# Two of four wq loads split into eight-row transfers and wider, fewer instructions around them, in a GQA decode and Mish layer on one Trainium2 core

## The chip, the cores and the metric

The kernel runs on one core of a Trainium2 chip. The metric is the time of one execution on the device in microseconds (us), as the median of some runs. PE is TensorE, DVE VectorE, ACT ScalarE, POOL GpSimd, SP SyncE; PEld stands for the weight loads of PE. The 16 DMA engines of the core bring all data from HBM.

## The reference, cut to what matters

The layer adds the input, a grouped-query attention over a cache, and a dense layer with Mish. One token for each of 8 batches, 512 features, 32 query heads over 8 heads of keys and values (4 queries each), 8192 cached positions, heads of 128, all in float32.

```python
xn = layernorm(x)                                  # x [8, 1, 512]
q = (xn @ wq).reshape(B, 1, 32, 128)               # wq [512, 4096]
k, v = repeat(k_cache, 4, axis=1), repeat(v_cache, 4, axis=1)   # [8, 8, 8192, 128] each
p = softmax(einsum("bhqd,bhkd->bhqk", q, k) * 128 ** -0.5)
a = einsum("bhqk,bhkd->bhqd", p, v).reshape(B, 1, 4096) @ wo    # wo [4096, 512]
h = xn @ w1 + b1                                   # w1 [512, 1792]
return x + a + (h * tanh(softplus(h))) @ w2        # w2 [1792, 512]
```

The caches are 268 MB each, so nearly all of the 561 MB that are read are keys and values.

## The kernel before

**Items and buffers.** The work is a list of items, each with a load and a function that works on the loaded tile. `buffer()` hands out four tiles of 128 x 32 KB (`BUFS = 4`), and the main loop at the end of the kernel calls the load of item i + 3 (`AHEAD = 3`) before it works on item i. All big loads are issued on SP, in this order; each waits until its buffer is free, that is until PE has read the item four places before. `load_rows` (L104) gives every partition one contiguous run, 32 KB for a k or v item (4 MB in all), 16 KB for a wq or wo item (2 MB). x_sb (8 rows of 2 KB) and b1_sb (4 rows of 1792 B) are loaded by ACT at the start.

**The order.** A pack p is half of the batches (`PB = 4`) of one key head: 16 packs. The list begins with wq item 0, then k items of pack p alternate with v items of pack p - 1. w1 comes after the second k item, three more wq items at the third batch of packs 2, 6 and 10, wo items between packs, and at the end w2 in three parts with the last wo item in two parts between them. `after(k, f)` puts f off by k steps; a step is a `yield` of an item, so small work on PE falls between the parts of the big items. PE, DVE and POOL each run their instructions in program order.

**What an item does.** A wq item i projects the queries of the key heads n = 2i and 2i + 1: `project` runs 16 small matmuls for each n (L271; 8 columns of weights, 128 of data, the four query heads into four groups of 32 partitions of H), `spread_q` scales and spreads q (L284), transposes it by matmuls against psel (L294) and copies it to qc (L301). `expand` masks it by row group into the block matrix qT (L319). `scores` multiplies qT with a k tile into S (L359; 32 MATMUL records of 128x512 for an item, each float32 matmul being recorded as two), and in the last batch of a pack takes the maximum (L370). `maximum` and `weights` turn S into exponents (L413), which two transposes on DVE bring to pt (L422). `values` multiplies pt with a v tile (L450) into one of two O banks by the parity of the batch, and DVE picks the diagonal blocks with four instructions per batch (L460 once, L462 three times), masks in isel. `merge` sums groups of rows (L477) and divides (L481), `turn` transposes the result of one head by 16 matmuls (L499) and copies it to oW (L507), and `outputs` multiplies oW with a wo tile (L530) and adds to acc (L540); for the last pair of heads it adds into H instead. `mish` and `down` (L597) are the dense layer; `down` adds into H. The last instructions add H and acc into res (L752) and store it (L753).

Of the kernel before, what the change touches and what calls it, by code (L numbers as in the profile page):

```python
# [60 lines left out]
QR = CC  # L61
OR = 4
# [9 lines left out]
def kernel(  # L72
# [76 lines left out]
    O = [psum.tile([P, 512], F32, name=f"o{i}") for i in range(2)]  # L149
# [7 lines left out]

    psel = const.tile([P, REP, B], F32, name="psel")
# [12 lines left out]

    half = const.tile([P, 2], F32, name="half")
    qT = [const.tile([P, PB * (QB + 1)], F32, name=f"qT{i}") for i in range(QBUFS)]
    qc = const.tile([P, 4, KR, REP, B], F32, name="qc")
    qc0 = const.tile([P, KA, REP, B], F32, name="qc0")

    xnT = const.tile([P, QR, B], F32, name="xnT")
    xw = const.tile([P, W1R, 2, B], F32, name="xw")
    acc = const.tile([P, P], F32, name="acc")
    aT = const.tile([P, 2 * W2R, Q], F32, name="aT")  # L180

    def setup():
# [5 lines left out]
        for o in O:  # L188
            nc.vector.memset(o, 0.0)

        st = const.tile([B, 8], F32, name="st")
        scratch = work.tile([P, TG, NH, P], F32, name="e", bufs=1).rearrange("p t s f -> p (t s f)")
# [19 lines left out]
        nc.vector.tensor_copy(xnT.rearrange("p r b -> p (r b)"), M[:, : QR * B])  # L212
# [4 lines left out]
        nc.vector.tensor_copy(psel, ident.rearrange("p (h q) -> p h q", h=REP)[:, :, :B])  # L217
# [17 lines left out]
        nc.vector.tensor_scalar(far, far, FAR, -FAR, op0=ALU.mult, op1=ALU.add)  # L235

# [9 lines left out]
        return wide  # L246
# [17 lines left out]
    q_at = [H[:, 384:512], H[:, 256:384]]  # L264

    def project(n, w):

        for r in range(QR):
            for h in range(REP):
                at = r * BW + (n % 2 * REP + h) * DH  # L270
                nc.tensor.matmul(  # L271
                    q_at[n % 2][Q * h : Q * h + B, :],
                    xnT[:, r, :],
                    w[:, at : at + DH],
                    start=(r == 0),
                    stop=(r == QR - 1),
                )

    def spread_q(n, k, copies, dst):

        qs = work.tile([P, KR * P], F32, name="qs", bufs=1)[:, : k * P].rearrange(
            "p (r g i) -> p r g i", r=k, g=copies
        )
        nc.vector.tensor_scalar_mul(  # L284
            qs,
            q_at[n % 2]
            .rearrange("p (i r o) -> p r o i", r=k, o=1)
            .to_broadcast([P, k, copies, DH // k]),
            DH**-0.5,
        )  # L290

        def transposed():
            for r in range(k):
                nc.tensor.matmul(  # L294
                    H[:, r * R : (r + 1) * R],
                    qs[:, r].rearrange("p g i -> p (g i)"),
                    psel.rearrange("p h b -> p (h b)"),
                    start=True,
                    stop=True,
                )  # L300
            nc.vector.tensor_copy(  # L301
                dst, H[:, : k * R].rearrange("p (r h b) -> p r h b", r=k, h=REP)
            )

        return transposed

    def expand(p):


        n, hb = divmod(p, NP)  # L310
        t = qT[p % QBUFS]
        if p > 0:
            t = t.rearrange("p (b c) -> p b c", b=PB)[:, :, :QB]
            t = t.rearrange("p b (r q) -> p b r q", r=KR)
            q = qc[:, n % 4, :, :, hb * PB : (hb + 1) * PB].rearrange("p r h b -> p b r h")
            for j in range(NB):
                g, s = divmod(j, NH)
                lo = g * R + s * PB
                nc.vector.tensor_scalar(  # L319
                    t[:, :, :, lo : lo + R - U + 1 : U], q, bsel[:, j : j + 1], None, op0=ALU.mult  # L320
                )
# [55 lines left out]
    def maximum(p):  # L377
# [10 lines left out]
        nr2 = work.tile([1, REP, NH, PB], F32, name="nr2")  # L388
        for s in range(NH):
            nc.vector.tensor_copy(nr2[:, :, s, :], nb)  # L390
        nx = NX[p] = work.tile([1, G, R], F32, name="nx")
        nc.vector.tensor_copy(
            nx,
            nr2.rearrange("p h s b -> p (h s b)")
            .rearrange("p (o q) -> p o q", o=1)
            .to_broadcast([1, G, R]),
        )

    def weights(p):
# [3 lines left out]
        nc.tensor.transpose(M[:, 128:129], NX.pop(p).rearrange("p g q -> p (g q)"), ident[:1, :1])  # L403
# [16 lines left out]
        half = TG // 2  # L420
        for i in range(2):
            nc.vector.transpose(  # L422
                pt.rearrange("p (m t r) -> p t m r", m=TW, t=TG)[:, half * i : half * (i + 1)],
                e.rearrange("p t s (q m) -> p t m (s q)", m=TW)[:, half * i : half * (i + 1)],
            )
# [16 lines left out]
    def values(p, b, vt):  # L442
# [16 lines left out]
        os = OS[p, b] = work.tile([P, DH], F32, name="os", bufs=3)  # L459
        nc.vector.tensor_scalar(os, o[:, :DH], isel[:, 0:1], None, op0=ALU.mult)  # L460
        for i in range(1, W4):
            nc.vector.scalar_tensor_tensor(  # L462
                os,
                o[:, DH * i : DH * (i + 1)],
                isel[:, i : i + 1],
                os,
                op0=ALU.mult,
                op1=ALU.add,
            )
# [3 lines left out]
    def merge(p, b):  # L473
# [4 lines left out]
        if b == PB - 1:  # L478
            if hb == 0:
                oT[n] = work.tile([P, REP, B], F32, name="oT")  # L480
            nc.vector.tensor_mul(  # L481
                oT[n][:, :, hb * PB : (hb + 1) * PB],
# [3 lines left out]
            if hb == NP - 1:  # L486
                after(1, lambda: turn(n))

    def turn(n):


        if n % 2 == 0:
            oW[n] = work.tile([P, OR, 2, B], F32, name="oW")
        to = oW[n - n % 2]
        o = oT.pop(n)
        for k in range(2):
            j = n % 2 * 2 + k
            for r in range(OR):
                nc.tensor.matmul(  # L499
                    M[Q * j : Q * (j + 1), 384 + r * 2 * B : 384 + (r + 1) * 2 * B],  # L500
                    ident[:, r::OR],
                    o[:, 2 * k : 2 * k + 2, :].rearrange("p h b -> p (h b)"),
                    start=True,
                    stop=True,
                )
        rows = slice(n % 2 * 64, n % 2 * 64 + 64)
        nc.vector.tensor_copy(  # L507
            to[rows].rearrange("p r h b -> p (r h b)"), M[rows, 384 : 384 + OR * 2 * B]
        )

    def outputs(n, w, lo=0, hi=OR):


        last = n == HKV - 2
        to = H[:, :P] if last else M[:, 256:384]
        if n == 0:

            for g in range(G):
                nc.tensor.matmul(
                    to[Q * g : Q * g + B, :],  # L520
                    ident[:B, :B],
                    x_sb[:, g * P : (g + 1) * P],
                    start=True,
                    stop=False,
                )
        for r in range(lo, hi):
            for h in range(2):
                for g in range(G):
                    at = r * BW + h * D + g * P
                    nc.tensor.matmul(  # L530
                        to[Q * g : Q * g + B, :],
                        oW[n][:, r, h, :],
                        w[:, at : at + P],
                        start=(r == 0 and h == 0 and 0 < n and not last),
                        stop=(r == OR - 1 and h == 1 and not last),
                    )
        if n == 0:
            nc.vector.tensor_copy(acc, to)
        elif not last:
            nc.vector.tensor_add(acc, to, acc)  # L540

    def mish(w1_sb):
# [29 lines left out]
        one = work.tile([P, FG], F32, name="mo", bufs=1)  # L572
# [20 lines left out]
    def down(lo, hi, w):  # L593
        for j in range(2 * lo, 2 * hi):
            for g in range(G):
# [5 lines left out]
                    start=(j == 0),  # L601
# [17 lines left out]
    def wq_item(i):  # L619
        def spread(n):  # L620
            return spread_q(n, KR, NB, qc[:, n % 4])

        def work_on(t):
            project(2 * i, t)
            if i == 0:

                first = spread_q(0, KA, KA, qc0)
                project(1, t)
                first()

                def rest():
                    spread(0)()
                    after(1, lambda: spread(1)())

                after(2, rest)
            else:
                project(2 * i + 1, t)
                even = spread(2 * i)

                def then():  # L640
                    even()
                    after(1, spread(2 * i + 1))

                after(2, then)
# [166 lines left out]
```

## Time and profile before

| | |
|---|---|
| median of 3 runs | 1317.86 us (1317.59 to 1318.09) |
| the profiled execution | 1317.59 us, of which the profile's span is 1315.7 us |
| instructions in the profile | 11664: PE 5268 MATMUL and 5268 LDWEIGHTS, DVE 679 |
| busy | PE 1197.2 us (91%), DVE 275.5 us (21%), ACT 40.1 us (3%), POOL 10.9 us (1%) |
| DMA | 561.82 MB, 427 GB/s on average; 325 in the last of 40 slices |
| mean granted TensorE clock | 0.984 |

How to read it: matmuls are pipelined, so the mean duration of one (L359: 606 ns) is more than its share of the busy time (868.7 us for 1920). A chip's DMA engine works through packets, here of 4 to 32 KB; the records of the packets name their queue, start, length and size, and not the engine. A 4-byte packet is the increment of a semaphore, one on each engine that a transfer used.

### The profile page before, as it was taken

What the parts mean: (1) busy time and instruction counts of PE and PEld (TensorE: products, weight loads), DVE (VectorE), ACT (ScalarE), POOL (GpSimd) and SP (SyncE); (2) the same over time, 40 slices, a digit from 0 to 9 for tenths busy, and PEclk for the clock granted to TensorE, in tenths of its full rate; (3) what the DMA queues carried; (4) which work ended last, traced back from release to release, by engine and by line L of the source; (5) the groups of instructions that cost most, each with busy time, mean ns of one, the idle gap of its engine ahead of it and who ended that gap; (6) DMA issues with size and microseconds to landing.
All of it is one profiled execution on the core that took longest, in us unless ns stands there. A gap on an engine that the chain in (4) does not pass through costs nothing.

```text
span 1315.7 us, 11664 instructions
## 1 busy us (share of the span) xinstructions
PE 1197.2 (91%) x5268; PEld 514.7 (39%) x5268; DVE 275.5 (21%) x679; ACT 40.1 (3%) x68; POOL 10.9 (1%) x13
## 2 busy tenths in 40 slices
PE   4999989999988998999989999899999998999986
PEld 2333344434333334443334434444343433434332
DVE  5430311303021031120303012121120301203021
ACT  0000000000000000000000000000000000000000
POOL 3000000000000000000000000000000000000000
PEclk9999999999999998999999999899999999999988
DMA  9999999999999999999999999999999999999997
GB/s 401 428 430 430 432 430 430 430 431 432 432 429 430 430 428 432 430 431 430 431 430 429 433 433 426 433 430 433 430 432 430 428 432 430 430 431 431 430 430 325
DMA packets 21033, 561.82 MB, mean 427 GB/s; under 512 B 2284, under 2 KB 2416, under 8 KB 2552
## 3 DMA queue, kind: packets, MB, share of 16 engines
q1 hardware_dynamic: 20960, 561.06, 99.4%
q8 instruction: 41, 0.67, 0.2%
q14 instruction: 8, 0.07, 0.0%
q10 hardware_dynamic: 24, 0.02, 0.0%
HBM read 561.01 MB, written 0.07 MB: 426 GB/s over the span
## 4 chain that ended last, share of the span: by engine, by line
PE 50%; DMA 47%; DVE 2%; issue 0%; ACT 0%; SPq 0%; ACTq 0%; DVEq 0%
DMA kv<-in_kT 45%; PE s L359 41%; PE o L450 6%; DMA kv<-in_w 2%; PE h L294 1%; PE s L346 1%; DVE gsel L214 1%; PE m L477 0%; PE m L499 0%; PE m L403 0%; ACT e L413 0%; DVE qT L319 0%; DVE pt L422 0%; PE m L530 0%; PE h L271 0%
## 5 line engine op out<-in xcount | busy, mean ns | idle before, releaser
L359 PE MATMUL s<-kv,qT 128*128 128x512 f32 x1920 | 868.7, 606 | 78.5 <-DMA kv<-in_kT 78.5
L359 PEld LDWEIGHTS s<-kv,qT 128*128 128x128 f32 x1920 | 358.8, 192 | 522.6 <-issue 427.2
L450 PE MATMUL o<-kv,pt 128*32 128x512 f32 x2048 | 241.8, 608 | 13.6 <-DMA kv<-in_v 7.3
L460 DVE TENSOR_SCALAR os<-o,isel 128x128 f32<-128x128 f32 x64 | 22.5, 351 | 605.3 <-PE o L450 605.3
L450 PEld LDWEIGHTS o<-kv,pt 128*32 128x32 f32 x2048 | 73.7, 139 | 156.2 <-issue 137.8
L413 ACT ACTIVATE e<-s,nms 128x1024 f32<-128x1024 f32 x32 | 35.3, 1109 | 1180.6 <-DVE nms L407 1180.6
L422 DVE STREAM_TRANSPOSE pt<-e 128x1024 f32<-128x1024 f32 x32 | 63.1, 2010 | 39.2 <-ACT e L413 39.2
L462 DVE SCALAR_TENSOR_TENSOR os<-o,isel,os 128x128 f32<-128x128 f32 x192 | 67.4, 351 | 6.8
L370 DVE TENSOR_REDUCE nm<-s 128x1 f32<-128x1024 f32 x16 | 19.6, 1225 | 212.4 <-PE s L359 211.3
L477 PEld LDWEIGHTS m<-hsel,os 128*128 128x128 f32 x128 | 23.7, 190 | 32.2 <-issue 30.5
L346 PE MATMUL s<-kv,qT 128*64 128x512 f32 x128 | 31.2, 644 | 1.5 <-issue 1.5
L319 DVE TENSOR_SCALAR qT<-qc,bsel 128x128 f32<-128x128 f32 x120 | 30.8, 340 | 0.2
L294 PEld LDWEIGHTS h<-psel,qs 128*128 128x128 f32 x136 | 17.2, 200 | 5.7 <-issue 4.6
L477 PE MATMUL m<-hsel,os 128*128 128x4 f32 x128 | 18.8, 217 | 0.0
L346 PEld LDWEIGHTS s<-kv,qT 128*64 128x64 f32 x128 | 9.7, 148 | 20.2 <-issue 20.1
L294 PE MATMUL h<-psel,qs 128*128 128x32 f32 x136 | 17.1, 280 | 0.2 <-DVE qs L284 0.2
L271 PE MATMUL h<-kv,xnT 128*8 128x128 f32 x256 | 9.6, 308 | 7.7 <-DVE qs L284 7.3
L301 DVE COPY qc<-h 128x256 f32<-128x256 f32 (+1 forms) x9 | 3.7, 410 | 58.7 <-PE h L294 58.7
L271 PEld LDWEIGHTS h<-kv,xnT 128*8 128x8 f32 x256 | 7.4, 99 | 10.7 <-DVE qs L284 7.8
L481 DVE TENSOR_TENSOR oT<-m,r 128x16 f32<-128x16 f32 x16 | 2.8, 174 | 39.0 <-PE m L477 39.0
L284 DVE TENSOR_SCALAR qs<-h 128x1024 f32<-128x1024 f32 (+1 forms) x9 | 10.4, 1161 | 0.7 <-PE h L271 0.7
L438 DVE RECIPROCAL r<-m 128x16 f32<-128x16 f32 x16 | 4.1, 257 | 29.4 <-PE m L434 29.4
(96 smaller groups left out, 160.3 us busy)
## 6 DMA issues: line engine op xcount, KB each, us to landing
kv<-in_kT SPq DMA_DIRECT2D x64, 4096.0 KB, 24.6
kv<-in_v SPq DMA_DIRECT2D x64, 4096.0 KB, 30.3
kv<-in_wq SPq DMA_DIRECT2D x4, 2048.0 KB, 19.1
kv<-in_wo SPq DMA_DIRECT2D x3, 2048.0 KB, 25.9
kv<-in_w SPq DMA_DIRECT2D x1, 3584.0 KB, 35.6
kv<-in_w SPq DMA_DIRECT2D x1, 2048.0 KB
kv<-in_wo SPq DMA_DIRECT2D x2, 1024.0 KB, 22.2
kv<-in_w SPq DMA_DIRECT2D x1, 1024.0 KB, 22.2
```

Of the source, the lines that this page charges most:

```text
L271: nc.tensor.matmul(q_at[n % 2][Q * h : Q * h + B, :], xnT[:, r, :], w[:, at : at + DH], start=(r == 0), stop=(r == QR - 1),)
L294: nc.tensor.matmul(H[:, r * R : (r + 1) * R], qs[:, r].rearrange("p g i -> p (g i)"), psel.rearrange("p h b -> p (h b)"), start=True, stop ...
L319: nc.vector.tensor_scalar(t[:, :, :, lo : lo + R - U + 1 : U], q, bsel[:, j : j + 1], None, op0=ALU.mult)
L346: nc.tensor.matmul(sp[WK * z : WK * (z + 1), cols], t[:, w : w + WK], k[:, z, at : at + 512], start=(b == 0 and i == 0), stop=(b == PB - 1 ...
L359: nc.tensor.matmul(sp[:, cols], t[:, w : w + P], k[:, at : at + 512], start=(b == 0 and r == 0), stop=(b == PB - 1 and r == KR - 1),)
L370: nc.vector.tensor_reduce(NM[p], sp, axis=AX.X, op=ALU.max, negate=True)
L413: nc.scalar.activation(e[:, :, s, :], S[p % 2].rearrange("p (t f) -> p t f", t=TG), AF.Exp, bias=nms[:, s : s + 1], accum_out=l[:, s : s + 1],
L422: nc.vector.transpose(pt.rearrange("p (m t r) -> p t m r", m=TW, t=TG)[:, half * i : half * (i + 1)], e.rearrange("p t s (q m) -> p t m (s ...
L450: nc.tensor.matmul(o[Q * c : Q * (c + 1), :], PT[p][:, W4 * R * j + b : W4 * R * (j + 1) : PB], vt[:, 512 * j : 512 * (j + 1)], start=(k = ...
L460: nc.vector.tensor_scalar(os, o[:, :DH], isel[:, 0:1], None, op0=ALU.mult)
L462: nc.vector.scalar_tensor_tensor(os, o[:, DH * i : DH * (i + 1)], isel[:, i : i + 1], os, op0=ALU.mult, op1=ALU.add,)
L477: nc.tensor.matmul(M[:, at : at + REP], OS.pop((p, b)), hsel, start=True, stop=True)
```

## The change

- `project` takes one matmul per row block with all four heads as its 512 columns (weights are xnT, copied four times side by side), into H for even n and into the first O bank for odd n.
- wq items 2 and 3 are loaded otherwise: the first 128 of the 512 rows of a block go to partitions 0 to 31, four rows (16 KB) each, in four transfers of eight partitions; the other 384 rows go to all partitions, three rows (12 KB) each, in one transfer. `project` then runs four matmuls over 32 partitions and three over 128.
- `spread_q` scales, transposes on DVE, and masks by half; `expand` copies by column group (four instructions for eight).
- `weights` makes one transpose of 2048 columns of two of 1024.
- `values` masks and adds the o of two batches at once, after the odd one: a multiplication over both O banks and a sum over the four blocks. The last two batches of the last pack are done one by one. `merge` follows for both.
- `turn` is done for two heads at once, with 4 matmuls and 4 copies. `outputs` uses 512 columns into H and acc has 512 columns; `add_up` brings acc into H before `down`; the last instruction copies H.

```diff
+SPLIT = P
+SR = QR - 1
...
-    O = [psum.tile([P, 512], F32, name=f"o{i}") for i in range(2)]
+    OO = psum.tile([P, 2, 512], F32, name="o")
+    O = [OO[:, i] for i in range(2)]
...
+        nc.vector.memset(xnT, 0.0)
+        nc.vector.memset(xnS, 0.0)
...
+    def setup_split(xc):
+        for r in range(SR):
+            nc.tensor.transpose(
+                M[:, 32 + r * B : 32 + (r + 1) * B], xc[:, SPLIT + r :: SR], ident[:B, :B]
+            )
+        nc.vector.tensor_copy(
+            xnS[:, :, :, :B],
...
+    q_at = [H, O[0]]
+
+    def project(n, w, split):
+
+        rows = [(xnT[:, r], w[:, r * BW : (r + 1) * BW]) for r in range(QR)]
+        if split:
+            k = SPLIT // QR
+            rows = [(x[:k], y[:k]) for x, y in rows]
+            rows += [(xnS[:, r], w[:, (QR + r) * BW : (QR + r + 1) * BW]) for r in range(SR)]
+        for r, (x, y) in enumerate(rows):
+            nc.tensor.matmul(
+                q_at[n % 2],
+                x.rearrange("p g q -> p (g q)"),
+                y[:, n % 2 * D : (n % 2 + 1) * D],
+                start=(r == 0),
+                stop=(r == len(rows) - 1),
+            )
+
+    def spread_q(n, k):
...
+        for g in range(copies):
+            nc.vector.tensor_scalar_mul(
+                qs.rearrange("p (h r g i) -> p h r g i", h=REP, r=k, g=copies)[:, :, :, g],
+                q_at[n % 2].rearrange("p (h i r) -> p h r i", h=REP, r=k),
+                DH**-0.5,
+            )
+        nc.vector.transpose(qt, qs)
...
+        for s in range(NH):
+            nc.vector.tensor_scalar(
+                qc[:, n % 2, :, :, :, s],
...
     def expand(p):
...
+            for g in range(G):
+                rows = slice(Q * g, Q * (g + 1))
+                nc.vector.tensor_copy(
+                    t[rows, :, :, g * R : (g + 1) * R - PB + 1 : PB], q[rows]
                 )
...
+        last = p == PACKS - 1 and b >= PB - 2
+        if b % 2 == 0 and not last:
+            return
+        lo, n = (b % 2, 1) if last else (0, 2)
+        o = OO[:, lo : lo + n].rearrange("p b (i d) -> p b i d", i=W4)
+        nc.vector.tensor_mul(
+            o, o, isel.rearrange("p (b i d) -> p b i d", b=1, d=1).to_broadcast([P, n, W4, DH])
+        )
+        os = work.tile([P, 2, DH], F32, name="os")
+        nc.vector.reduce_sum(os[:, :n], o.rearrange("p b i d -> p b d i"), axis=AX.X)
...
     def wq_item(i):
-        def spread(n):
-            return spread_q(n, KR, NB, qc[:, n % 4])
+        split = i >= HKV // 2 - 2
...
+            project(2 * i, t, split)
             if i == 0:
 
-                first = spread_q(0, KA, KA, qc0)
...
+                spread_q(0, KA)
+                expand(0)
+            project(2 * i + 1, t, split)
+            spread(2 * i)
+            after(2, lambda: spread(2 * i + 1))
             yield
 
-        return lambda: load_rows(wq[i * CC : (i + 1) * CC]), work_on
+        def load():
+            src = wq[i * CC : (i + 1) * CC]
+            if not split:
+                return load_rows(src)
+            src = src.rearrange("j p f -> (j p) f")
+            t = buffer()
+            first = src[:SPLIT].rearrange("(p r) f -> p (r f)", r=QR)
+            for q in range(4):
+                nc.sync.dma_start(t[q : SPLIT // QR : 4, : QR * BW], first[q::4])
+            nc.sync.dma_start(
+                t[:, QR * BW : (QR + SR) * BW],
+                src[SPLIT:].rearrange("(p r) f -> p (r f)", r=SR),
+            )
+            return t
+
+        return load, work_on
```

More of the change, by code (lines that the diff above doesn't have):

```diff
@@ L260, in setup_w1 @@
             )
[L264 to L302, printed above, removed]
-            )
-        return transposed
@@ L419, in weights @@
             )
[L420 to L425, printed above, removed]
+        nc.vector.transpose(
+            pt.rearrange("p (m t r) -> p t m r", m=TW, t=TG),
+            e.rearrange("p t s (q m) -> p t m (s q)", m=TW),
+        )
         ls = work.tile([P, 1], F32, name="ls")
@@ L485, in merge @@
             )
-            if hb == NP - 1:
-                after(1, lambda: turn(n))
+            if odd and hb == NP - 1:
+                after(1, lambda: turn(pair))
     def turn(n):
[L492 to L497, printed above, removed]
+        to = oW[n] = work.tile([P, OR, 2, B], F32, name="oW")
+        o = oT.pop(n).rearrange("p n h b -> p (n h b)")
@@ new lines, in turn @@
+        cols = 2 * REP * B
+        for r in range(OR):
+            nc.tensor.matmul(
+                M[:, 256 + r * cols : 256 + (r + 1) * cols],
+                tid[:, r].rearrange("p g i -> p (g i)"),
+                o,
+                start=True,
+                stop=True,
+            )
+        m = M[:, 256 : 256 + OR * cols].rearrange("p (r j q) -> p j r q", r=OR, j=G)
+        for j in range(G):
+            rows = slice(Q * j, Q * (j + 1))
+            nc.vector.tensor_copy(
+                to[rows].rearrange("p r h b -> p r (h b)"), m[rows, j]
+            )
@@ L498, in turn, with outputs @@
+    def outputs(n, w):
+        if n == 0:
+            nc.tensor.matmul(H[:B, :], ident[:B, :B], x_sb, start=True, stop=False)
+        for h in range(2):
             for r in range(OR):
+                at = r * BW + h * D
                 nc.tensor.matmul(
[L500 to L504, printed above, removed]
-                )
@@ L506, in turn @@
[L506 to L515, printed above, removed]
-        if n == 0:
[L518 to L525, printed above, removed]
+                    H[Q * r : Q * r + B, :],
@@ new lines, in outputs, with add_up @@
+                    oW[n][:, r, h, :],
+                    w[:, at : at + D],
+                    start=(h == 0 and (n, r) != (0, 0)),
+                    stop=(h == 1),
+                )
+        if n == 0:
+            nc.vector.tensor_copy(acc, H)
+        else:
+            nc.vector.tensor_add(acc, H, acc)
+    def add_up():
+        for g in range(G):
+            nc.tensor.matmul(
+                H[Q * g : Q * g + B, :P],
+                rsel[:, :B],
+                acc[:, g * P : (g + 1) * P],
+                start=True,
+                stop=False,
+            )
@@ L750 @@
     assert not late
[L751 to L752 removed]
+    res = acc[:, :P]
+    nc.vector.tensor_copy(res, H[:, :P])
     nc.sync.dma_start(out, res)
```

141 lines of the change are left out of this document (68 added, 73 removed).

## The prediction

> **What bounds the kernel now.** I read four things in this order: the page's slices and DMA queues, the timeline of the last 18 us, the issues of the DMA queue around the third wq load, and the trace's packet records.
>
> From the page (busy tenths in 40 slices; then queue, kind: packets, MB, share of 16 engines):
>
> ```profile
> PE   4999989999988998999989999899999998999986
> DVE  5430311303021031120303012121120301203021
> DMA  9999999999999999999999999999999999999997
> q1 hardware_dynamic: 20960, 561.06, 99.4%
> q8 instruction: 41, 0.67, 0.2%
> q14 instruction: 8, 0.07, 0.0%
> ```
>
> All 16 DMA engines are busy from start to end, PE nearly so. The tensors come on q1. q8 and q14 are small, but they are the code of the engines, and they ride on the same DMA engines.
>
> The last instructions (start, length, engine, line, idle before and releaser):
>
> ```profile
> 1306.82 0.93 PE L499 MATMUL m<-oT,ident 128*32 128x16 f32 x16 [0.27 <-DVE oT L481]
> ...
> 1311.09 1.06 PE L530 MATMUL h<-kv,oW 128*8 128x128 f32 x32 [1.08 <-DMA kv<-in_wo]
> 1312.34 0.62 PE L597 MATMUL h<-kv,aT 128*8 128x128 f32 x16 [0.19 <-DMA kv<-in_w]
> 1313.03 0.29 DVE L752 TENSOR_TENSOR res<-h,acc 128x128 f32<-128x128 f32 x1 [5.01 <-PE h L597]
> 1313.35 0.35 SPq L753 DMA_DIRECT2D out<-res  x1
> ```
>
> PE waits for the last part of w2, and what follows is fixed. So the time is the landing of that part on the **last** DMA engine.
>
> The packet records (queue, start, length, bytes; no engine) show which one that is. A packet starts about 4 ns before the one ahead of it on its engine ends, so engines can be followed as chains, and each load ends on each engine in a packet of 4 bytes, its semaphore. On the leading engine these follow each other by 9.72 us per 4 MB, with one lapse of 0.2 us: it never starves otherwise. The last part of w2 lands on the sixteen engines at 1304.453 us plus, in ns:
>
> ```
> 0 110 275 338 455 726 1510 4869 | 7236 7415 7680 7727 7732 7775 7784 7841
> ```
>
> Eight engines are 7.2 to 7.8 us late. Each q8 packet (16 KB, 1.02 to 1.10 us) shifts one engine for good: the fetch at 152.7 us moves the engine at offset 687 ns to 2237, the one at 184.3 us another from 587 to 2137, 1.55 us each. Eight engines take turns (lengths of the packets repeat every eighth time), 40 fetches came before the end, five each. PE ran 10316 instructions between the first and the 41st fetch, 258 per fetch. [...] The engine at 4869 had five q14 fetches of 0.97 us, one per 128 to 135 DVE instructions.
>
> **The change, part by part.**
>
> *Fewer PE instructions.* Each matmul stands as two MATMULs and two LDWEIGHTS, a transpose as one of each. Of the 5268 MATMULs L271 goes from 256 to 88 (two unsplit items of 8 matmuls, two split ones of 14), L294's 136 go, turn has 32 for 128, the earlier outputs 50 for 200, add_up brings 8, the three new transposes 3: 4729, with weights 9458 instructions for 10536. That is 1078/258, four fetches less: 37, the last near the end. The engines of turns 1 to 4 keep five, those of turns 7 and 8 have four. DVE's records fall from 679 to about 432 (256 of os become 66, 120 of expand 60, pt and nx 16 less each, spread_q 25 more, turn 8 more): three q14 fetches that count, not five, 1.9 us off that engine.
>
> *The split loads, the term that decides.* Per split load eight engines get four packets of 16 KB and eight of 12 KB, the others eight of 12 KB only, in place of eight of 16 KB for all. A 16 KB packet steps by 0.607 us, one of 8 KB by 0.309, so one of 12 KB by 0.458 (estimate, between the two). High side: 8 x 0.458 = 3.66 for 4.86, -1.2 us. Low side: 3.66 + 4 x 0.607 + four more ends of about 10 ns = 6.13, +1.25. Two loads: **-2.4 us on eight engines, +2.5 us on eight**.
>
> Which eight? x_sb is a transfer of eight rows, b1 of four. x_sb's semaphore packets end at 1.78 to 2.17 us, and five wq packets start right behind (6 or 7 ns after these packets start), at 1.782, 1.798, 1.799, 1.812 and 2.172 us. b1's four rows lie in the chains that begin at 1.812, 1.819, 2.123 and 2.181. That makes eight chains. A second mark agrees: every fourth packet is 7 ns longer (621 for 614), and exactly the eight other chains share one phase of it. Followed on, the chains from 1.798 and 1.799 have the offsets 0 and 190 ns at the first load, and those two jump at the fetches of 238.4 and 205.8 us: turns 8 and 7. So of the eight that the change loads, six fetch no PE code and **two do**; of the eight that it relieves, six do. [...]
>
> Sum on the two (four fetches stand in the trace at load 134: 5.64 and 5.82 us): 5.82 + 2.5 = 8.3. The relieved six: 7.84 - 2.4 = 5.4. DVE's code engine: 4.87 - 1.9 + 2.5 = 5.5. The last landing moves from 7.84 to about 8.35: **+0.5 us**.
>
> *PE around the wq loads.* What stands there now:
>
> ```profile
> 828.38 1.93 PE L271 MATMUL h<-kv,xnT 128*8 128x128 f32 x64
> 830.37 0.33 SPq L104 DMA_DIRECT2D kv<-in_v  x1
> 835.35 6.64 PE L359 MATMUL s<-kv,qT 128*128 128x512 f32 x8 [4.72 <-DMA kv<-in_kT]
> 841.83 1.87 PE L294 MATMUL h<-psel,qs 128*128 128x32 f32 x16
> 855.89 0.33 SPq L104 DMA_DIRECT2D kv<-in_kT  x1
> ```
>
> A split item has 28 passes of 128x512. L359's 1920 take 868.7 us, 0.452 each: 12.7 us for 1.93. PE then ends the item at 841.1, and since it did not idle, the k item takes 3.7 + 10.8 = 14.5 and ends at 855.6; today it ends at 855.8. The next k load is issued as before. The load at 830.37 goes out 10.7 us later; the slowest engine has 23.8 us of earlier packets left there, the fastest 17.3. The least that the slowest engine has ahead of it after the first load is 7.9 us, so none of this reaches it.
>
> *DVE.* os costs 64 x 351 + 192 x 351 ns = 90 us now. After: 31 pairs of 1024 columns masked and summed at 1.225 (L370) to 1.43 us (L576's 626 ns for 448 columns, scaled), and two single ones: 76 to 91 us, hidden behind k items of 14.5 us. Before the second projection O must be read: 2.9 us against 6.3 us of the first. spread_q takes the transposes from PE (16 x 2 us less) and is off every path. pt is needed whole: v(15,0) starts 1.9 us later, at 1276.6, and its second half of v(15,1) ends at 1287.9, before v(15,2) lands (1288.97). At the end turn's four copies for one add 0.6 us; oW is ready at 1308.9, the last wo part lands after 1311: hidden. Setup gains 0.9 us of memsets; the fifth load has 15.4 us of cover. Zero for all of these; without cover the end would pay the 0.6.
>
> *Small transfers.* Near the end 1 MB loads step by 2.49 us on the leading engine, for 9.72/4 = 2.43: 0.06 each, within the 2.5 above. [...]
>
> The profiled execution took 1317.59 us for a span of 1315.7; the median is 1317.86. With +0.5 on both: 1318.1 and **1318.4**.
>
> **The rivals.**
>
> *The two code engines are not among the eight loaded ones.* All fetching engines would be relieved: the end goes to 5.4 or 5.5, -2.4 us, 1315.5. Against it: the two marks of the chains above; for it: they are marks of two small transfers on another queue, and the change's kernel is another program whose turns may lie elsewhere. 2.4 is just under the bound of 0.2% (2.64 us; about what a measurement of this kernel can tell from no change), and a fetch less on the last engines takes it past. Chance 0.28.
>
> *The two keep five fetches*, the turns beginning two engines further on: 7.42 + 2.5 = 9.9, +2.1 us, 1319.9. The eight first turns speak against. 0.09.
>
> *PE becomes the bound (slower).* After 4.7 us of idling eight passes took 6.64 us, 0.83 each. At that rate a split item takes 23.2 us, the k item ends at 866.1, 10.2 late. From issue to first packet about 1.7 us pass (with 1.48 us ahead of it the leading engine lost 0.2), so the slowest engine would starve for 10.2 - 6.3 = 3.9 us, and at the item before (9.6 ahead) for 2.7: with the 0.5 about 1325. It bites from 0.69 us a pass. PE comes busy from v items, which speaks against it. 0.06.
>
> *The eight-row transfers are spread over all 16 engines*: no shift, end near 7.8, 1317.9. x_sb's eight packets of 2 KB speak against. 0.07.
>
> **How the numbers follow.** My forecast has 0.50, its own range 1317.6 to 1319.2 (size of the 12 KB step, receipt times). The first rival puts half of its 0.28 past 0.2%: faster 0.15. Slower: PE's 0.06, some 0.04 from the upper ends of five fetches and the forecast. Same 0.75. The range goes from 1315.0 (the first rival with half a microsecond more) to 1320.0 (five fetches).
>
> **What would show it.** In the changed profile: 37 packets on q8; the sixteen ends of a load before the second split one apart from those after it by 1.2 us up on eight, down on eight; of the last landing's sixteen, two alone at 8.1 to 8.4 us behind today's 1304.45, the next group at 5 to 5.6. I am wrong if the last landing comes before 1310.5 (first rival), if the two stand at 9.9, or if the slowest engine's steps in the steady part exceed 9.72 us behind a wq load without a fetch (PE). L271's mean per pass shows the last directly.

## The result, and the profile after

The changed kernel takes 1320.01 us (median of 20 runs, 1317.94 to 1322.05), the kernel before, beside it, 1317.75 us (20 runs, 1317.56 to 1318.09): 2.3 us more. The ratio on record, which weighs all runs, is 1.0015 with a 95% interval of 1.0009 to 1.0022. That is under the 0.2% (2.64 us) at which the prediction draws its line, but the whole interval lies above 1, so the changed kernel is a little slower. The median stands 0.01 us above the top of the predicted range. The profiled execution took 1320.19 us for a span of 1318.3 (before: 1317.59 and 1315.7).

The page of the changed kernel: busy tenths, granted clock, DMA share, and then the DMA queues (packets, MB, share).

```profile
PE   6799999998988999999899999999999998998976
PEclk9999999999999999999999999899999999999988
DMA  9999999999999999999999999999999999999997
...
q1 hardware_dynamic: 21088, 561.06, 99.2%
q8 instruction: 37, 0.61, 0.2%
...
q14 instruction: 7, 0.06, 0.0%
```

DMA is as full as before. PE's code comes in 37 packets on q8 in place of 41, one q14 packet is gone.

The timeline of the last 5 us:

```profile
1313.68 1.06 PE L577 MATMUL h<-kv,oW 128*8 128x128 f32 x32 [0.88 <-DMA kv<-in_wo]
1314.94 0.62 PE L641 MATMUL h<-kv,aT 128*8 128x128 f32 x16 [0.20 <-DMA kv<-in_w]
1315.63 0.29 DVE L807 COPY acc<-h 128x128 f32<-128x128 f32 x1 [4.82 <-PE h L641]
1315.95 0.35 SPq L808 DMA_DIRECT2D out<-acc  x1
```

PE waits for the last w2 part at the end, as before, and what follows has the same length. The matmul stands at 1314.94 for 1312.34: all 2.6 us of the span are in the landing. The packet records give that landing on the sixteen DMA engines, 1308.782 us plus (ns):

```
0 36 129 344 349 819 842 1809 1978 2144 2722 3098 3147 3503 | 4358 6112
```

Two engines stand behind the others, the last at 1314.894, where before eight stood together and the last was at 1312.294. So +2.60 us on the last landing is the whole difference.

The timeline around the third wq load, and the issues behind it:

```profile
828.28 3.70 PE L307 MATMUL h<-kv,xnT 32*128 32x512 f32 x8
...
831.90 4.54 PE L307 MATMUL h<-kv,xnS 128*128 128x512 f32 x6
836.37 4.33 PE L307 MATMUL o<-kv,xnT 32*128 32x512 f32 x8
...
840.63 5.49 PE L307 MATMUL o<-kv,xnS 128*128 128x512 f32 x6
...
846.15 0.33 SPq L107 DMA_DIRECT2D kv<-in_v  x1
...
860.40 0.33 SPq L107 DMA_DIRECT2D kv<-in_kT  x1
```

The split item lasts from 828.28 to 845.9, 17.6 us, and the next k load is issued at 860.40 (before: 855.89). The windows of those four groups (window, length, busy by engine, granted clock, DMA share, GB/s):

```profile
828.30:831.80 3.50, 3.50 (x12) 1.38 (x8) 2.46 (x2) 0.00 (x0) 0.00 (x0) 1.00 0.96 412
831.90:836.30 4.40, 4.40 (x7) 1.60 (x6) 0.00 (x0) 0.00 (x0) 0.00 (x0) 0.61 1.04 443
836.40:840.60 4.20, 4.20 (x9) 1.37 (x8) 3.32 (x5) 0.00 (x0) 0.00 (x0) 0.85 1.04 445
840.70:845.90 5.20, 5.20 (x7) 2.12 (x7) 0.00 (x0) 0.00 (x0) 0.00 (x0) 0.50 0.96 411
```

PE is busy without a gap, yet its granted clock falls to 0.61 and 0.50 in the groups that follow the matmuls of 32 rows. The leading DMA engine runs dry 20 us later: its landings fall back by 5.7 us about 867 us, and the spread from the first to the last engine shrinks from 8.79 to 3.06 us. Thirteen of the sixteen engines then land within 0.65 us of each other; the last three go on by 9.72 us per 4 MB.

### The profile page after: what moved, and what is told of

The parts are those of the page before. It is cut to its first block, busy times and chain, and to the rows that moved or that the text cites. A ratio compares the mean times of both kernels' runs of the same rounds, so it can differ in the third digit from the quotient of the medians.

```text
span 1318.3 us, 10372 instructions
## 1 busy us (share of the span) xinstructions
PE 1211.2 (92%) x4729; PEld 504.0 (38%) x4729; DVE 272.1 (21%) x432; ACT 40.1 (3%) x68; POOL 10.9 (1%) x13
## 3 DMA queue, kind: packets, MB, share of 16 engines
q1 hardware_dynamic: 21088, 561.06, 99.2%
## 4 chain that ended last, share of the span: by engine, by line
PE 50%; DMA 48%; DVE 2%; issue 0%; ACT 0%; SPq 0%; ACTq 0%; DVEq 0%
DMA kv<-in_kT 46%; PE s L391 40%; PE o L476 6%; DMA kv<-in_w 2%; PE h L307 1%; PE o L307 1%; PE s L378 1%; DVE gsel L233 1%; DVE pt L448 0%; PE m L505 0%; ACT e L441 0%; DVE o L491 0%; DVE os L495 0%; PE m L460 0%; DVE o L202 0%
## 5 line engine op out<-in xcount | busy, mean ns | idle before, releaser
L391 PE MATMUL s<-kv,qT 128*128 128x512 f32 x1920 | 857.3, 602 | 67.1 <-DMA kv<-in_kT 67.0
L491 DVE TENSOR_TENSOR o<-o,isel 128x1024 f32<-128x1024 f32 (+1 forms) x33 | 39.6, 1200 | 383.8 <-PE o L476 383.8
L448 DVE STREAM_TRANSPOSE pt<-e 128x2048 f32<-128x2048 f32 x16 | 62.1, 3879 | 39.2 <-ACT e L441 39.2
L495 DVE TENSOR_REDUCE os<-o 128x256 f32<-128x1024 f32 (+1 forms) x33 | 39.3, 1192 | 1.1
L351 DVE COPY qT<-qc 32x256 f32<-32x256 f32 x60 | 23.1, 385 | 0.7
L307 PE MATMUL h<-kv,xnT 128*128 128x512 f32 (+1 forms) x32 | 16.6, 665 | 0.4 <-DVE xnT L226 0.4
L307 PE MATMUL o<-kv,xnT 128*128 128x512 f32 (+1 forms) x32 | 15.2, 617 | 0.0
L326 DVE STREAM_TRANSPOSE e<-e 128x1024 f32<-128x1024 f32 (+1 forms) x9 | 10.7, 1186 | 0.3
L307 PEld LDWEIGHTS h<-kv,xnT 128*128 128x128 f32 (+1 forms) x32 | 6.4, 210 | 9.8 <-issue 9.3
L460 PEld LDWEIGHTS m<-lsel,ones 128*128 128x128 f32 x32 | 5.9, 190 | 8.3 <-issue 7.5
```

Source lines behind the costliest of these rows:

```text
L307: nc.tensor.matmul(q_at[n % 2], x.rearrange("p g q -> p (g q)"), y[:, n % 2 * D : (n % 2 + 1) * D], start=(r == 0), stop=(r == len(rows) - 1),
L351: nc.vector.tensor_copy(t[rows, :, :, g * R : (g + 1) * R - PB + 1 : PB], q[rows])
L391: nc.tensor.matmul(sp[:, cols], t[:, w : w + P], k[:, at : at + 512], start=(b == 0 and r == 0), stop=(b == PB - 1 and r == KR - 1),)
L448: nc.vector.transpose(pt.rearrange("p (m t r) -> p t m r", m=TW, t=TG), e.rearrange("p t s (q m) -> p t m (s q)", m=TW),)
L491: nc.vector.tensor_mul(o, o, isel.rearrange("p (b i d) -> p b i d", b=1, d=1).to_broadcast([P, n, W4, DH]))
L495: nc.vector.reduce_sum(os[:, :n], o.rearrange("p b i d -> p b d i"), axis=AX.X)
```

## The experiments

In the expectations, A is the prediction's theory: the end is the last landing, set by the bytes and the code packets on one DMA engine, and the split loads move it. B is its rival: PE's or DVE's rewritten work, or the slower split items, set the time. C names one part of B: the granted clock that falls in the split items starves the DMA engines. R was formed later: the first turn of PE's code fetches lies on another engine in each execution. "Low" and "lowest" name the engines that the transfers of eight and of four rows go to, as names only.

**The changed kernel with whole loads.**

```diff
-        split = i >= HKV // 2 - 2
+        split = False
```

> The changed kernel with all four wq loads whole again (one transfer of 2 MB each), all else as changed. Theory A (the eight-row transfers load two engines that also carry PE code): the last landing is set by an engine with four or five code fetches and no shift, 1317.0 to 1318.0 us, and the granted clock stays at 1.0 in all wq items. Theory B (the new work on PE and DVE costs the time, the loads do not): it stays at 1319.5 to 1320.5. Theory C (the clock falling to half in the split items starves the DMA engines): also 1317 to 1318, so C and A part on the next run.

Measured: 1317.56 us, before 1317.64, ratio 1.0002 (0.9993 to 1.0011).

```profile
1312.42 0.62 PE L641 MATMUL h<-kv,aT 128*8 128x128 f32 x16 [0.20 <-DMA kv<-in_w]
```

In its timeline the last w2 matmul is back at 1312.42, the last landing at 1312.375, while its q8 count is the changed kernel's 37. The split loads alone make the 2.3 us; the 563 MATMULs fewer (4705 for 5268), the os of two batches and the rest of the rewrite neither cost nor gain anything that can be measured. B falls for all but the split items.

**One load split.**

```diff
-        split = i >= HKV // 2 - 2
+        split = i >= HKV // 2 - 1
```

> The changed kernel with only the last of the four wq loads split. Theory A: half of the two loads' shift: +1.25 us on the low engines against the same kernel without a split (1317.56 us): 1318.7 us, within 0.4. Rival (the loss comes from the starved stage at the last wq load and its slow passes alone): the whole 2.4 us, 1320 us. Second rival (it comes from the earlier split load): 1317.6 us.

Measured: 1318.70 us (1316.95 to 1320.60), ratio 1.0009 (1.0001 to 1.0018), as A said: half. At the split load the slowest landing steps by 0.75 us against the kernel with whole loads and the leading one by -1.2.

**The split loads alone, in the kernel before.** The load and seven row groups in the old projection:

```diff
+            k = SPLIT // QR
+            rows = [(x[:k], y[:k]) for x, y in rows]
+            rows += [(xnS[:, r], w[:, (QR + r) * BW : (QR + r + 1) * BW]) for r in range(SR)]
...
+            for q in range(4):
+                nc.sync.dma_start(t[q : SPLIT // QR : 4, : QR * BW], first[q::4])
```

> The kernel before with the change's split wq loads alone (their seven row groups go through the old projection of 8 columns by 128, so no wide passes, no shared o tile, no masks of two batches). Theory A: the two low engines that carry PE code keep five fetches each (192 PE instructions more make no sixth round for them) and get +1.25 us per split load: 7.24 + 2.5 to 7.84 + 2.5, 9.7 to 10.3 us behind the leading landing, 1319.8 to 1320.3 us; about 1.2 us of it appear at the second wq load, 1.2 at the third. Rival (the wide passes at half the TensorE clock and the later issues behind them make the loss): no difference from the kernel before, 1317.7 us.

Measured: 1318.80 us, ratio 1.0014 (1.0005 to 1.0023): slower without any wide pass, but by 1.2 us, not by the 2.2 to 2.7 that were expected. The sixteen landings are 1306.082 plus:

```
0 182 286 351 376 453 936 2300 2348 2493 2653 2881 2891 4534 | 7074 7608
```

Two alone again, with the six relieved code engines far ahead of them. What is missing lies in another place: each 4 MB load takes 9.713 us on this kernel's leading engine (median of 123 steps) and 9.720 on that of the other kernels, 0.9 us over the run. Why it streams 0.07% faster was not found. Its runs fall in two groups, seven at 1318.46 to 1318.89 and four at 1320.31 to 1321.04 (taken up below the table).

**Bytes on the eight low engines, and nothing else.** A load that nobody reads, into the unused half of one wo buffer of the kernel before:

```diff
+            if n == 2:
+                again = wq[:CC].rearrange("j p f -> (j p) f")[:P].rearrange("(p r) f -> p (r f)", r=CC)
+                for q in range(4):
+                    nc.sync.dma_start(t[q : 32 : 4, OR * BW :], again[q : 32 : 4])
```

> The kernel before, to which one load is added that nobody reads: four transfers of eight rows of 16 KB to every fourth partition of 0 to 31, into the unused half of a wo buffer. Theory A: four packets of 0.607 us more, +2.43 us, on the eight low engines, and nothing on the others; the two low ones that carry PE code (five fetches each, as all have) end 9.2 to 10.2 us behind the leading landing in place of at most 7.84: 1319.0 to 1320.0 us, all runs close together. Rival (the eight engines loaded carry no PE code): the others still set the end, no change, 1317.6 us. If partitions 0 to 31 crowded as 96 to 127 did, ten us or more would be lost.

Measured: 1320.04 us (1319.78 to 1320.45), ratio 1.0018 (1.0009 to 1.0026). Its queues and its last w2 matmul:

```profile
q1 hardware_dynamic: 21024, 561.59, 99.3%
q8 instruction: 41, 0.67, 0.2%
```

```profile
1314.58 0.62 PE L597 MATMUL h<-kv,aT 128*8 128x128 f32 x16 [0.20 <-DMA kv<-in_w]
```

0.53 MB more, four packets of 16 KB on each low engine. The landings: 1306.776 plus

```
0 11 91 140 143 934 1290 | 5142 5268 5270 5282 5314 5535 5560 | 7556 7764
```

The two at the end stand at 1314.33 and 1314.54, 2.25 us past the 1312.29 of before. The middle group of seven ends at 1311.9 to 1312.3, where the eight code engines ended before (1311.7 to 1312.3); it has room for the six that were not loaded and for DVE's. This is the prediction's picture: of PE's eight code engines two are low, and they set the end.

**The same with four rows.** `16` for `32` in the slices above.

> The kernel before with the same unread load of half the size: four transfers of four rows of 16 KB to every fourth partition of 0 to 15, so the four lowest engines get +2.43 us each. Theory A: none of the four carries PE code (the four rows of b1 lie on chains that take no turn), and DVE's code engine, if it is among them, ends at 4.87 + 2.43 = 7.3 us, under the 7.84 of the slowest: no change, 1317.6 us within 0.3. Rival (any load more on single engines shows at the end, or PE code lies there too): 1319 to 1320 us.

Measured: 1317.98 us (1317.73 to 1318.27), ratio 1.0002 (0.9994 to 1.0011). At most 0.3 us: 2.4 us more (four packets of 0.607) on these four engines do not reach the end, so none of the four carries PE's code.

**A whole row group for the slow passes.** GpSimd fills the rest of the first half with zeros, and the projection multiplies 128 rows:

```diff
-            rows = [(x[:k], y[:k]) for x, y in rows]
...
+            for lo, hi in ((SPLIT // QR, 64), (64, P)):
+                nc.gpsimd.memset(t[lo:hi, : QR * BW], 0.0)
```

> The changed kernel in which GpSimd writes zeros to partitions 32 to 127 of the split loads' first half, so the four row groups of 32 partitions are multiplied as 128 partitions (same number of passes, same loads, same result). Theory A: the slow passes and the lower granted clock of the split items (17.6 us for the second) come from the matmuls of 32 rows; here the items take 12 to 13 us at a granted clock of 1.0, and yet the time stays that of the changed kernel, 1319.5 to 1320.3 us, since the end hangs on the loads. Rival (the long split items make the loss): 1317.6 us. If the clock drops all the same, the rows of a matmul are not its cause.

Measured: 1319.84 us (1318.00 to 1321.88), ratio 1.0015 (1.0006 to 1.0023). Its timeline and windows of the same item:

```profile
827.84 3.70 PE L305 MATMUL h<-kv,xnT 128*128 128x512 f32 x8
...
831.38 2.74 PE L305 MATMUL h<-kv,xnS 128*128 128x512 f32 x6
833.96 3.60 PE L305 MATMUL o<-kv,xnT 128*128 128x512 f32 x8
...
837.39 2.74 PE L305 MATMUL o<-kv,xnS 128*128 128x512 f32 x6
```

```profile
831.40:833.90 2.50, 2.50 (x7) 1.12 (x6) 0.00 (x0) 0.00 (x0) 0.00 (x0) 1.00 0.98 419
834.00:837.30 3.30, 3.30 (x9) 1.48 (x8) 3.07 (x5) 0.00 (x0) 0.00 (x0) 1.00 1.05 442
837.40:839.90 2.50, 2.50 (x7) 1.13 (x6) 0.15 (x1) 0.00 (x0) 0.00 (x0) 1.00 0.97 419
```

The item takes 12.1 us at a granted clock of 1.0, 5.5 less than in the changed kernel; the spread of the landings stays at 8.56 us about 867 us, so almost nothing ran dry. The last landing is at 1314.454, 0.44 us earlier, and the median 0.17 us lower: the long split items are not where the 2.3 us went, and B falls here too, with it C. A few tenths of a microsecond can't be excluded, since the runs of both kernels spread over 4 us.

**As many code fetches as before.** Four small matmuls ahead of each k block of the changed kernel:

```diff
+            for _ in range(4):
+                nc.tensor.matmul(M[:REP, 200 : 200 + REP], hsel, hsel, start=True, stop=True)
```

> The changed kernel with four idle matmuls (4 by 4, on a free corner of PSUM) ahead of the scores of every k block: 256 matmuls, 1024 PE instructions more, so about 41 code fetches in place of 37, as many as the kernel before, and 40 ahead of the end. Theory R (the first turn of PE's code fetches lies on another of the eight engines in each execution, so with 36 fetches ahead of the end a low engine has five of them in five executions of eight and four in the others; the runs of the changed kernel fall into 1320.2 and 1318.5 us for that reason): with 40 every engine has five in every execution, so the low ones always end at 10.4 us, and all runs lie within 0.5 us of 1320.3 us, none near 1318.5. Rival (the PE instructions saved have nothing to do with the spread of the runs): median near 1320.0 with runs from 1318.0 to 1322.0 as before. Second rival (fewer PE instructions were a gain of their own): 1321 us or more in all runs.

Measured: 1325.03 us (1320.56 to 1330.46), ratio 1.0057 (1.0039 to 1.0076). The page's chain, and the added matmuls among its groups:

```profile
PE 77%; DMA 19%; DVE 3%; issue 1%; ACT 0%
...
L706 PE MATMUL m<-hsel 128*4 128x4 f32 x512 | 22.1, 166 | 36.4 <-DVE nr L413 36.4
```

This tells nothing of R. The matmuls write to M, and waited 36.4 us for DVE's reads of it; PE got 77% of the chain (50% in the changed kernel). The 36.4 us lie in fourteen waits of up to 2.6 us, and PE became the bound.

**Rows moved between engines in a v load.** Five kernels took rows 96 to 127 (or 112 to 127) of one v load in four transfers of eight (or four) rows. In the kernel before, eight rows:

```diff
+        nc.sync.dma_start(t[:96], rows[:96])
+        for q in range(96, P, 8):
+            nc.sync.dma_start(t[q : q + 8], rows[q : q + 8])
```

> The kernel before, with one single v load (4 MB, pack 4, first batch) in five transfers: partitions 0 to 95 in one, 96 to 127 in four of eight rows. The bytes per engine shift as in the change's two wq loads together (2.43 us each way), no work on any engine changes. Theory A: eight engines 2.4 us earlier, eight 2.4 to 2.5 later, among them two of the eight late ones, so the last landing is about 9.9 us behind the leading unshifted engine in place of 7.84: +2.1 us, 1319.8, with a narrow spread since all eight fetching engines have five. First rival of the prediction (the fetching engines are all relieved): -2.4 us, 1315.4. Theory C: no change, 1317.75.

Four rows, in the kernel before and in the changed one with whole loads:

> The kernel before, with one single v load in five transfers: partitions 0 to 111 in one, 112 to 127 in four of four rows. Four engines get 3.65 us more, twelve 1.2 us less. Theory A: the four of b1 carry no PE code, one of them DVE's code (4.87 us late); it comes to 8.5, the eight fetching ones to 6.6: +0.7 us, 1318.4, and in the trace six of the eight late engines stay together with the two, all eight 1.2 us earlier. If PE code were fetched by any of the four: 11.5, +3.6 us, 1321.4.

> The first of these kernels (changed, wq loads whole) with the four-row transfers of the third in one v load. Theory A: DVE's code engine has only three or four fetches here, 2.9 + 3.65 = 6.6 or 7.5, the fetching eight 6.6 or less: -1.0 us against the kernel before, 1316.7 (1316.2 to 1317.4). Theory B: as the first of these kernels, 1319.5 or more.

Measured: 1343.52, 1338.27 and 1338.84 us; ratios 1.0193 (1.0179 to 1.0207), 1.0154 (1.0140 to 1.0168) and 1.0162 (1.0148 to 1.0176). All three lie 20 to 24 us above what was expected. I took the adjacent partitions for the cause and wrote to every fourth one, as the change does, with `t[96 + q :: 4]` and `t[112 + q :: 4]`:

> The kernel before, in which one v load (pack 4, batch 0) comes as one transfer of partitions 0 to 95 and four transfers of eight rows of 32 KB, now to every fourth partition of 96 to 127, as the changed kernel's small transfers write, not to adjacent ones. Nothing else differs. Theory A (the end is the last landing on the engine with most bytes and code): eight engines get ten rows and eight get six, in place of eight: four packets of 0.607 us more, +2.43 us, on the two low engines that carry PE code; they end 9.7 to 10.2 us behind the leading landing, and the kernel takes 1319.7 to 1320.1 us. If the crowding of adjacent partitions was what cost the 26 us of the earlier form, the eight-row transfers end within 5 us of each other here. Rival (no PE code on the eight loaded engines): the relieved engines set the end, 1315.3 us. Second rival (any small transfer of rows of 32 KB is slow, whatever its partitions): about 1343 us again.

> The changed kernel with all four wq loads whole, in which one v load (pack 4, batch 0) comes as one transfer of partitions 0 to 111 and four transfers of four rows of 32 KB to every fourth partition of 112 to 127. Theory A: twelve engines get seven rows for eight (-1.2 us), the four that b1's transfer uses get eleven (+3.64 us). PE's code engines, none of them among the four, end 6.6 us behind the leading landing in place of 7.76; DVE's, with two or three fetches of 0.97 us, at most 6.6 as well. So 1.2 us below the kernel with whole wq loads: 1316.4 us. If DVE's code engine or one of PE's is among the four and fuller than I take it, 1318 to 1320 us. Rival (the end hangs on PE and not on single engines): no difference, 1317.6 us.

Measured: 1334.21 and 1332.05 us; ratios 1.0124 (1.0110 to 1.0138) and 1.0111 (1.0097 to 1.0125). Better by 7 to 9 us, and still far off. The windows of the first of the two, during that load and after it:

```profile
386.00:410.00 24.00, 16.72 (x123) 8.63 (x121) 7.64 (x18) 2.30 (x4) 0.00 (x0) 0.91 1.05 222
420.00:444.00 24.00, 20.07 (x74) 8.12 (x70) 1.40 (x4) 0.00 (x0) 0.00 (x0) 0.93 1.00 429
```

222 GB/s for 429: most packets of 32 KB take 2.3 to 2.6 us in place of 1.22. The first 90 or so of them, from 386 to 401 us, do so already; by the order of issue they are those of the transfer of 96 rows. So the small transfers are not the whole price, and these kernels lost on a price of their own and decide nothing between A and B; the two unread loads, to partitions 0 to 31 and 0 to 15, do.

## Why the prediction was right, and where it failed

The time stayed within 0.2%, as forecast, but narrowly: the sum had +0.5 us, and the measured 2.3 us stand just under the line of 2.64. That they do is luck, since one step of the sum failed; the rest of the mechanism held.

The bound was named rightly: in every profiled run but those of the v-load kernels and of the one with small matmuls added, the time is the last landing and 5.2 to 5.7 us. The counts hold: 37 packets on q8, 4729 MATMULs, 432 DVE instructions. The masks and sums of os took 39.6 + 39.3 = 79 us, within 76 to 91, and their zero on the path is shown by the kernel with whole loads (-0.08 us).

**The split term was sized rightly, and on the right engines.** +2.5 us was worked out for the low eight (2.55 by its own terms); the changed kernel ends 2.52 us behind the same kernel with whole loads (1314.894 and 1312.375). The four packets of 16 KB alone gave 2.25 in the kernel before, for 4 x 0.607 = 2.43. That two of the eight loaded engines fetch PE code, read from two marks in the first microseconds, is shown by the two unread loads: eight rows cost 2.4 us, four rows at most 0.3. That the split loads' eight-row transfers use the same eight engines as x_sb's eight rows was my estimate from those marks; no run shows it for each of the eight. The rival that had the code engines elsewhere falls, and so does the one that spread the transfers over sixteen.

**The step that failed is "those of turns 7 and 8 have four".** The fetches go round the eight engines in a fixed order, a ring: in the kernel before the first eight packets took 1074, 1069, 1061, 1099, 1099, 1087, 1026 and 1018 ns, and lengths within 11 ns of these come again in every round. But the first turn of the changed kernel was another than that of the kernel before. By the order of the packet lengths the ring begins here (numbered by the turns of the kernel before):

| kernel | q8 packets | first turn | loads | lowest to highest run, us |
|---|---|---|---|---|
| before | 41 | 1 | whole | 1317.56 to 1318.09 |
| four rows unread | 41 | 3 | whole | 1317.73 to 1318.27 |
| eight rows unread | 41 | 6 | low +2.4 | 1319.78 to 1320.45 |
| whole loads | 37 | 8 | whole | 1317.40 to 1317.80, one at 1320.78 |
| one load split | 37 | 8 | one split | 1316.95 to 1320.60 |
| changed | 37 | 8 | two split | 1317.94 to 1322.05 |
| zeros, 128 rows | 37 | 8 | two split | 1318.00 to 1321.88 |
| before, split | 42 | 5 | two split | 1318.46 to 1321.04 |

The changed kernel's ring began one engine earlier, so the low engine that I had as turn 8 became turn 1 and kept five fetches; the other kept four. The trace has just that: the fetch at 1172 us moves the landing of one of the two last engines from 2.8 to 4.4 us behind the leading one, and the 33rd, at 1208.06 us, that of the other from 4.6 to 6.1; none comes after on either. At the end the two are 1.75 us apart, about one fetch of 1.55, at 8.7 and 10.4 us behind the leading landing of before. The first is the 8.3 of my forecast, the second the 9.9 that I priced as the rival of five fetches, at 1319.9 us and a chance of 0.09. Both stand 0.4 to 0.5 us further back than priced, which no run explains. In the kernel before it makes no odds which turn is first, since 40 fetches give every engine five; with 36 ahead of the end four engines have five and four have four, and the low pair escapes five in three of eight starts.

That the start differs between kernels with the same count of packets (1, 3 and 6) is shown. What fixes it, and whether it moves between executions of one kernel and so makes the spread of its runs, stays open, for each kernel has one trace, and the kernel meant to test it ran into PE. For the second of these, the theory R: if all eight starts were equally likely in each execution, 5 in 8 runs should stand near 1320.2 and the others near 1318.5; of the 31 runs of the two kernels with 37 packets and two split loads 21 lie above 1319.2 and 10 below 1319. The two groups of the kernel before with split loads would fit as well: with 41 fetches ahead of its end one engine has six, and in two of eight starts that is a low one.

Against R: all four traces of kernels with 37 packets in the table begin at 8, for which equal places give a chance of 1 in 512; with one load split only one run of eleven is near 1317, where three in eight are due; and the runs at 1322.05 and, with whole loads, at 1320.78 belong to no group. (The kernels with changed v loads or added matmuls began at 1, 1, 2, 2, 3 and 5; two of them have 37 packets.) The granted clock does not part the groups either: in the changed kernel it is 0.979 to 0.988 for the six runs below 1319 and 0.977 to 0.988 for the others. With eight equal places for the start the forecast would have been 1320 with 5 in 8, and 1318.4 with 3 in 8.

**PE's split item was undersized.** I had 28 x 0.452 = 12.7 us and a k load at 855.6; it took 17.6, with the load at 860.40, about halfway to the rival in which PE becomes the bound (0.83 us a pass, 1325 us). The unpriced part is the granted clock of 0.5 to 0.61. What hid it is what the prediction named, the packets that the slowest engine has ahead of it: the last three engines did not run dry (they went on by 9.72 us per 4 MB), and the kernel with 128 rows has a median only 0.2 us lower. It also explains why the relieved engines do not stand at 5.4 as predicted: they were among those that ran dry. In the kernel before with split loads, where they did not, they end at 1308.4 to 1309.0, before the 1309.9 of the forecast.

## What to carry to other kernels

With the DMA engines full (packets on q1 for 99.2% of their time) the end was set here by one engine and not by their mean: list the sixteen ends of a late landing before moving bytes, and count the code fetches as bytes (1.55 us each on their engine here). A small transfer that lands on a few engines cost nearly nothing (at most 0.3 us) or nearly all of its length (2.4 us) here, depending on what else those engines carried; an unread load of the same shape tells which. An order read from one trace (a first turn, a phase) need not hold for the changed kernel: give its other places their chances, above all when a count stops being a multiple of the ring.

No version here beats both kernels: the rewrite with whole loads equals the kernel before, and one load split gave a single run below all others (1316.95 us) but a median of 1318.70.

## What the runs showed of the hardware

**Behind matmuls of 32 rows TensorE's granted clock fell, though PE was never idle.** In the second split item the granted clock went from 1.00 to 0.61 behind the first 3.5 us of them, and to 0.50 behind the next group; in the first split item it fell to 0.61 behind the first group and stayed at 1.00 behind the second, so it did not fall each time. With zeros in the other 96 rows all four groups of the second item ran at 1.00, and the six passes behind each group took 2.74 us in both items. In the changed kernel PE was busy for the whole of each of these windows (4.40 of 4.40 us at 0.61, 5.20 of 5.20 at 0.50), so idle time of PE does not account for the drop. Only the rows in use, and GpSimd's zeros ahead of them, differ here; what lowers the clock was not shown.

**Which partitions a small transfer wrote mattered here.** Four transfers of eight rows cost 9.3 us less to every fourth partition of 96 to 127 than to adjacent ones (1334.21 and 1343.52 us). Transfers of eight rows to every fourth partition of 0 to 31 ran at full rate (0.61 to 0.62 us for 16 KB, as in whole loads), to every fourth of 96 to 127 at half (2.5 us for 32 KB, for 1.22), to adjacent ones of 96 to 127 most packets of 32 KB took 3.8 to 5.6 us. From 386 to 410 us the kernel with every fourth partition moved 222 GB/s, the kernel before 434. No run varied the partitions alone with the small transfers unmixed, and the transfer of 96 rows ran at half rate ahead of the small ones, so what slows them was not shown.

**Code fetches were data traffic of single engines.** In the traces before and after, a q8 packet of 16 KB shifted one engine by about 1.55 us for good (in the changed kernel the one at 1172 us from 2.8 to 4.4 us behind the leading engine, the one at 1208.06 from 4.6 to 6.1). Which of the eight engines begins the round differed between kernels (1, 3, 5, 6 and 8 in the table); what fixes it was not found.
